# Attention with a token and channel mixer on one core: seven products in more places, tails of two pairs together, a new order of work

## The chip, the core and the metric

The kernel runs on one core of a Trainium2 chip. Its engines are TensorE (PE; the loading of its stationary operand is shown as PEld), VectorE (DVE), ScalarE (ACT), GpSimd (POOL) and SyncE (SP); POOL and SP here only issue transfers (DMA). TensorE reads from the on-chip memory SBUF and writes to eight banks of PSUM, each 128 partitions by 512 float32 columns; DVE and ACT read the banks and write results back to SBUF. Every engine works through its own list in order, and an instruction that waits holds up all that stand behind it on the same engine.

The metric is the device time of one execution in microseconds (us). The kernel before took 278.68, 279.0 and 279.62 us in three runs; the median is 279.0 us.

## The reference

There are 8 batches of 576 rows, 8 heads of 64 columns. First comes causal attention in a window of 128 rows with a distance penalty per head; then the heads are put side by side to `x` (576 by 512 per batch), and a mixer follows, first over the rows, then over the columns:

```python
scores = scale * q @ k.T + slopes * -abs(i - j)     # only where 0 <= i - j < 128
attn = softmax(scores) @ v                          # per head
x = heads of attn side by side                      # (8, 576, 512)
h = np.maximum(x.T @ w_tok1, 0.0) @ w_tok2          # 576 -> 256 -> 576
u = x + h.T
h2 = np.maximum(u @ w_ch1, 0.0) @ w_ch2             # 512 -> 1536 -> 512
out = u + h2
```

Inputs and output are float32 in HBM; the kernel computes in bfloat16 with float32 sums.

## The kernel before

A batch has 576 rows: four blocks of 128 and a tail of 64. Two batches form a pair, and the two tails of a pair share one block of 128 rows (`TAIL`). The work of batch b is in two parts. `side(b)` is everything up to `u`: transposes of q and k, `scores` (L678 on PE, exponentials on ACT at L701, masks on DVE at L711), `values` (L745, then reciprocals and scaling on DVE at L758 and L761), `token_mix` (L790, L800, L833, L829, then the addition to `ub` at L851), and the transposed copy `uT` of `u` (from batch 2 on by SP as a transposing transfer, L859). `main(b)` is the channel mixer: a first layer 512 to 1536 with ReLU into `r2`, and a second layer 1536 to 512, whose result is added to `u` and stored.

The first layer is done in 12 chunks (`chunk`, L1030): each is four matmuls of 512 columns into one bank, followed by one ReLU (ACT L1036 or DVE L1037). In batch 7 alone it is done by `unit` (L952): a unit stands for four chunks. Like Strassen's scheme it cuts the 2 by 2 blocks of the product into seven products of half size instead of eight: 28 matmuls of 256 columns instead of 16 of 512. It pays for that with sums: four differences of `uT` per batch (`halves`, L916), in each unit three copies out of PSUM (`keep`, L967), three additions (`join`, L976) and three ReLUs (L978 or L980), and the last product's own ReLU (L996). The sums of the weights are made once (`hidden_sums`, L594). `UNITS` says how many of a batch's three units are done this way: three in batch 7, none elsewhere. Batches are counted from 0 here.

The second layer of the four full blocks is done by seven products in every batch (`second`, L1218; the last product of batch 7 at L1247), with sums of `r2` on DVE (`second_sums`, L1055), sums of the weights (`weight_sums`, L576), and seven additions to `u` (L1186). The tail block of a pair is done in the odd batch: its first layer by `tail_piece` (L1073: 16 matmuls of 128 columns, three times per pair; ReLU at L1078), its second layer by 12 plain matmuls of 512 columns (L1118; in batch 7 24 of 256), then the addition at L1125 and a store.

What sets the order: `Plan` collects all operations with an estimated cost, their buffers and a rank, and simulates the five engines. Whenever an engine comes free it takes the ready operation with the smallest rank, and the order thus found is written out as the program. `side(b+1)` has ranks that lay it over the first 38% of `main(b)`. Every rank gets a random shift of at most `SHIFT` from a seed per batch (`SEEDS`). The constants `START`, `CASTS`, `LATE`, `FETCH`, `PACKET` are the planner's assumptions on transfers; they move no transfer by themselves. The order in which q, k, v and the weights are asked for in the first pair is written by hand (`LOADS`); A0 to A3 are quarters of `w_ch1`, B0 to B3 quarters of `w_ch2`, W1, P1, W2 and T0 are the token weights. All of these go through POOL's queue. Where the planner's PE is idle in the first 60 us, `emit` puts in matmuls on a zero tile (`spin`, L1302), which keep TensorE from being idle and compute nothing.

Eight banks of PSUM, six buffers `ob` (used by stores and by `keep`) and two buffers `r2` are shared out in the simulation too.

Of the kernel before, what the change touches and what calls it, by code (L numbers as in the profile page):

```python
# [64 lines left out]

class Plan:
    def __init__(self):
        self.rings, self.ops, self.orders, self.part = {}, [], 0, 0
# [7 lines left out]
    def op(self, eng, cost, emit, rank, makes=(), adds=(), part=None, uses=(), reads=(), needs=(),  # L76
# [4 lines left out]
        o = Op()  # L81
# [3 lines left out]
        o.n = len(self.ops)  # L85
        o.deps = set(many(needs))
# [31 lines left out]
    def run(self):  # L118
        ops = self.ops
        dice = [random.Random(x) for x in SEEDS]  # L120
        for o in ops:
            if SEEDS[o.part]:
                o.rank += dice[o.part].uniform(-SHIFT, SHIFT)
# [177 lines left out]
    def emit(self, spin):  # L301
# [11 lines left out]
        for _, _, go in sorted(work, key=lambda w: w[:2]):  # L313
# [23 lines left out]
SEEDS = [45795, 495947, 190309, 331881, 0, 67117, 67408, 179769, 445757]  # L337
SHIFT = 1500.0
UNIT_LATE = False
SECOND_LATE = True  # L340
# [7 lines left out]
UNITS = [0, 0, 0, 0, 0, 0, 0, 3]  # L348
# [17 lines left out]
LOADS = ("q2 k2 k1 q1 v0 W2 k8 q8 v2 v1 v3 v8 W1 q7 k7 A0 P1 k5 q5 k4 v5 "  # L366
         "q4 A1 v4 k6 q6 A2 v7 v6 A3 T0 B0 B1 B2 B3")
# [3 lines left out]
def kernel(  # L371
# [57 lines left out]
    ring("v", AHEAD, [P, H, 2 * D])  # L429
# [4 lines left out]
    ring("ub", 2, [P, NB, DM])  # L434
# [4 lines left out]
    ring("uTt", 1, [P, NCB, P])  # L439
    ring("r2", 2, [P, NHT, NC * P])  # L440
    ring("r2t", 1, [P, NHT, P])
# [98 lines left out]
    lw1, lw2, lw2t, lc1, lc2 = [], [], [], [], []  # L540
    for item in LOADS.split():
        what, n = item[:-1], int(item[-1])
        if what in ("q", "k", "v"):
            load(what, 0, n, parts_of(0, n))
        elif what == "W":
            if n == 1:
                lw1 += weights([(W1[:, 0:NC, :], w1, 512, 2080)] +
                               [(W1p[0:R, 0, :], moe_w_tok1[NC * P : S, :], 64, 210)])
            else:
                lw2 += weights([(W2[:, :, :], w2[:, :, 0 : NC * P], 256, 2630)])  # L550
        elif what == "P":
            lw1 += weights([(W1p[R:P, 1, :], moe_w_tok1[NC * P : S, :], 64, 210)])
        elif what == "T":
            lw2t += weights([(W2t[:, :, :], w2[:, :, NC * P : S], 256, 300)])
        elif what == "A":
            hs = slice(n * DCH // 4, (n + 1) * DCH // 4)
            lc1 += weights([(WC1[:, :, hs], c1[:, :, hs], 512, 2500)]) * (NHT // 4)
        else:
            js = slice(n * NHT // 4, (n + 1) * NHT // 4)
            lc2 += weights([(WC2[:, js, :], c2[:, js, :], 384, 2680)]) * (NHT // 4)  # L560
# [52 lines left out]
    qkT, xbs, ubs, r1s, uts, wides = {}, {}, {}, {}, {}, []  # L613
    turned, marks, turns = {}, {}, {}
# [159 lines left out]
    def token_mix(b, rank):  # L774
# [38 lines left out]
        uTt = plan.buf("uTt") if half else None  # L813
# [3 lines left out]
        for blk in blocks:  # L817
# [29 lines left out]
            if fold:  # L847
                plan.op("ACT", 600, lambda blk=blk, ht=ht, hs=hs: act_.copy(out=ub()[:, blk, :], in_=ht()[:, hs]),
                        rk, part=(ub, blk), uses=[ht])
            else:  # L850
                plan.op("DVE", 690, lambda blk=blk, ht=ht, hs=hs: dve_.tensor_tensor(  # L851
                    out=ub()[:, blk, :], in0=ht()[:, hs], in1=xb()[:, blk, :], op=ALU.add), rk,
                    part=(ub, blk), uses=[ht], reads=tks)
        for blk in blocks:
            if b >= FROM_U:
                def turn(blk=blk):
                    c = blk % NC
                    to = uTt()[:, :, :] if blk == TAIL else uT()[:, :, c * P : (c + 1) * P]
                    nc.sync.dma_start_transpose(out=to, in_=ub()[:, blk, :])  # L859

                turned.setdefault(b, []).append(plan.op(
                    "SP", 1200, turn, rank(0), part=(uTt if blk == TAIL else uT, blk), reads=[(ub, blk)], bus=1000))
                continue
            ut = bank()

            def go(blk=blk, ut=ut):
                for cb in range(NCB):
                    pe_.transpose(ut().bitcast(BF16)[:, cb * P : (cb + 1) * P],  # L868
                                  ub()[:, blk, cb * P : (cb + 1) * P], ident[:, :])

            def copy(blk=blk, ut=ut, eng=dve_.tensor_copy):
                c = blk % NC
# [465 lines left out]
```

## Time and profile before

| | value |
|---|---|
| runs | 278.68, 279.0, 279.62 us; median 279.0 us |
| profiled execution: span from first to last instruction | 277.5 us |
| median less that span | 1.5 us |
| mean granted TensorE clock | 0.999 |
| PE busy, share of the span | 269.9 us, 97% |
| DVE / ACT / POOL busy | 209.6 / 139.8 / 114.0 us |
| matmuls in all | 2827 |
| of these on the zero tile | 45 |

A row of groups reads: line, engine, operation, what it writes <- what it reads, shapes and count | busy us, mean ns of one | idle time before them and what ended it. Matmuls overlap, so the mean of one (379 ns for 512 columns) is its latency; what one costs in a dense stretch is read from the chain of work that ended last: so many us for so many instructions. A row of windows gives the stretch, its length, then busy time and count of PE, PEld, DVE, ACT and POOL, the granted clock, the DMA share and GB/s. In a row of the timeline stand start, duration, engine, line and operation, and in brackets the idle time before it and who ended it. In the rows of transfers the last number is the median time from issue to landing.

### The profile page before, as it was taken

To read this page: it belongs to the slowest core of one execution; us is meant where nothing else is said; L and a number is where in the kernel's file an instruction comes from. 1 tells how busy PE (TensorE), PEld (TensorE's weight loads), DVE (VectorE), ACT (ScalarE), POOL (GpSimd) and SP (SyncE) were. 2 spreads that over 40 slices of the span, in tenths; PEclk is the share of its full clock that TensorE was granted. 3 is DMA by queue.
4 is the path that set the end of the run, shared out by engine and by line. 5 is a ranking of instruction groups with operands and counts; after the bars stand their busy time and mean duration, and the time that the engine had idled before them with its cause. 6 is when DMAs were issued, how large, how long until landed. Compare 5 with 4: busy or idle time off the path is not lost.

```text
span 277.5 us, 7005 instructions
## 1 busy us (share of the span) xinstructions
PE 269.9 (97%) x2827; PEld 180.1 (65%) x2827; DVE 209.6 (76%) x497; ACT 139.8 (50%) x238; POOL 114.0 (41%) x144
## 2 busy tenths in 40 slices
PE   7899999999999999999999999999999999999994
PEld 3565765685686555595567655576667645689883
DVE  6577699978897569853989478763989549877983
ACT  5573894336960298207951096206860079105650
POOL 8889865940256037900585009600472220013000
PEclk9999999999999999999999999999999999999999
DMA  8999999999699999999899989999499750043014
GB/s 155 163 159 160 183 194 186 155 133 218 107 113 105 177 234 140 131 135 185 175 134 143 196 214 97 138 155 246 50 120 99 197 140 0 2 127 121 1 57 135
DMA packets 167553, 38.71 MB, mean 139 GB/s; under 512 B 155808, under 2 KB 166688, under 8 KB 167520
## 3 DMA queue, kind: packets, MB, share of 16 engines
q0 software_dynamic: 114032, 19.77, 92.1%
q1 hardware_dynamic: 51264, 17.83, 33.4%
q10 hardware_dynamic: 2224, 0.66, 1.2%
q8 instruction: 22, 0.36, 0.5%
q14 instruction: 11, 0.09, 0.1%
HBM read 35.85 MB, written 9.44 MB: 163 GB/s over the span
## 4 chain that ended last, share of the span: by engine, by line
PE 93%; DMA 2%; DVE 2%; ACT 1%; issue 0%; SPq 0%; DVEq 0%
PE ps L1218 26%; PE ps L1030 25%; PE ps L745 7%; PE ps L678 6%; PE ps L790 5%; PE ps L833 5%; PE ps L1073 4%; PE ps L1118 4%; PE ps L952 3%; DMA raw<-in_q_dram 2%; PE ps L1302 2%; PE ps L638 2%; PE ps L800 1%; PE ps L829 1%; PE ps L868 1%; PE ps L1015 1%
## 5 line engine op out<-in xcount | busy, mean ns | idle before, releaser
L1030 PE MATMUL ps<-uT,WC 128*128 128x512 bf16 x328 | 79.1, 379 | 0.4 <-DVE xb L761 0.4
L701 ACT ACTIVATE pe<-ps 128x1024 bf16<-128x1024 f32 (+1 forms) x76 | 63.5, 889 | 27.0 <-PE ps L678 25.7
L518 POOL DMA_DIRECT2D v<-in_v_dram x40 | 34.1, 857 | 92.7 <-PE ps L745 89.2
L1036 ACT ACTIVATE r<-ps 128x512 bf16<-128x512 f32 x75 | 44.4, 602 | 40.5 <-PE ps L1030 38.5
L1030 PEld LDWEIGHTS <-WC 128*128 128x128 bf16 x328 | 29.3, 98 | 30.1 <-issue 1.3
L711 DVE TENSOR_TENSOR pe<-pe,mask 128x1024 bf16<-128x1024 bf16 (+1 forms) x64 | 38.1, 608 | 7.2 <-ACT pe L701 6.8
L1218 PEld LDWEIGHTS <-r 128*128 128x128 bf16 x372 | 35.9, 98 | 7.2 <-issue 0.2
L518 POOL DMA_DIRECT2D qk<-in_k_dram x38 | 32.8, 870 | 3.6 <-DMA v<-in_v_dram 1.6
L518 POOL DMA_DIRECT2D qk<-in_q_dram x38 | 32.8, 868 | 2.7 <-DMA WC<-in_moe_w_ch_dram 1.0
L1218 PEld LDWEIGHTS <-s 128*128 128x128 bf16 x288 | 27.5, 98 | 6.0 <-issue 1.3
L761 DVE TENSOR_TENSOR xb<-ps,rt 128x256 bf16<-128x256 f32 (+1 forms) x72 | 29.2, 416 | 0.7
L745 PEld LDWEIGHTS <-pe 128*128 128x128 bf16 (+1 forms) x560 | 22.3, 98 | 8.7 <-DVE pe L711 2.2
L745 PE MATMUL ps<-v,pe 128*128 128x65 bf16 (+1 forms) x560 | 26.2, 194 | 0.2 <-DVE pe L711 0.2
L1218 PE MATMUL ps<-WC,r 128*128 128x256 bf16 x192 | 25.4, 273 | 0.0
L1218 PE MATMUL ps<-WT,s 128*128 128x256 bf16 x192 | 24.6, 273 | 0.0
L851 DVE TENSOR_TENSOR ub<-ps,xb 128x512 bf16<-128x512 f32 x34 | 21.2, 681 | 1.8 <-PE ps L833 1.8
L1218 PE MATMUL ps<-WT,r 128*128 128x256 bf16 x180 | 22.4, 272 | 0.0
L678 PEld LDWEIGHTS <-qkT 64*128 64x128 bf16 x560 | 14.7, 94 | 11.1 <-issue 9.4
L1186 DVE TENSOR_TENSOR raw<-ps,ub 128x512 f32<-128x512 f32 x21 | 14.3, 685 | 9.1 <-PE ps L1218 8.9
L678 PE MATMUL ps<-qkT 64*128 64x128 bf16 (+1 forms) x304 | 19.4, 216 | 0.0
L1078 ACT ACTIVATE r2t<-ps 128x512 bf16<-128x512 f32 x12 | 7.2, 603 | 22.5 <-PE ps L1073 22.5
L758 DVE RECIPROCAL rt<-ps 128x4 f32<-128x4 f32 (+1 forms) x76 | 12.4, 174 | 6.8 <-PE ps L745 6.3
(105 smaller groups left out, 350.7 us busy)
## 6 DMA issues: line engine op xcount, KB each, us to landing
out_dram<-raw SPq DMA_DIRECT2D x17, 256.0 KB, 2.6
v<-in_v_dram POOLq DMA_DIRECT2D x32, 128.0 KB, 5.4
qk<-in_q_dram POOLq DMA_DIRECT2D x30, 128.0 KB, 5.6
qk<-in_k_dram POOLq DMA_DIRECT2D x30, 128.0 KB, 5.4
WC<-in_moe_w_ch_dram POOLq DMA_DIRECT2D x8, 384.0 KB, 9.1
out_dram<-ob SPq DMA_DIRECT2D x6, 256.0 KB, 2.6
out_dram<-ob POOLq DMA_DIRECT2D x4, 256.0 KB, 3.1
out_dram<-raw POOLq DMA_DIRECT2D x4, 256.0 KB, 2.9
```

The costliest lines, as they stand in the source:

```text
L518: nc.gpsimd.dma_start(out=to()[p0 : p0 + n, :, :], in_=rows(src, b, s0, n))
L678: pe_.matmul(wide(e)[:, i, kind, a:z], lhsT=ts[kb]()[e * D : (e + 1) * D, NHP + i, :], rhs=ts[blk]()[e * D : (e + 1) * D, i, a:z], start=n ...
L701: act_.activation(out=pb()[:, e, :, lo:, c0:c1_], in_=wide(e)[:, :, lo:, c0:c1_], func=ACT.Exp, scale=scale)
L711: dve_.tensor_tensor(out=o, in0=o, in1=heads(mk, es), op=ALU.mult)
L745: pe_.matmul(view()[a:z, at, i, :], lhsT=pb()[:, e, i, kind, a:z], rhs=vb()[:, h, 0 : D + 1], start=m == 0, stop=m == len(mms) - 1, skip_g ...
L761: dve_.tensor_tensor(out=x4(), in0=view()[r0:r1_, :, :, 0:D], in1=rt()[r0:r1_, 0:n, :, :].broadcast_to([r1_ - r0, n, 4, D]), op=ALU.mult)
L790: pe_.matmul(t1[j]()[:, :], lhsT=W1[:, c, j * P : (j + 1) * P], rhs=xb()[:, blk, :], start=c == 0, stop=False)
L851: plan.op("DVE", 690, lambda blk=blk, ht=ht, hs=hs: dve_.tensor_tensor(out=ub()[:, blk, :], in0=ht()[:, hs], in1=xb()[:, blk, :], op=ALU.a ...
L1030: pe_.matmul(ct()[:, :], lhsT=WC1[:, cb, t * P : (t + 1) * P], rhs=uT()[:, cb, :], start=cb == 0, stop=cb == NCB - 1)
L1036: plan.op("ACT", 600, lambda t=t, ct=ct: act_.activation(out=r2()[:, t, :], in_=ct()[:, :], func=ACT.Relu), rk, part=(r2, t), uses=[ct], o ...
L1186: dve_.tensor_tensor(out=v, in0=both(bk), in1=src, op=ALU.add)
L1218: pe_.matmul(of(bk, c), lhsT=l(t, c), rhs=w(t), start=first, stop=g == 1 and t == HK - 1, skip_group_check=True)
```

## The change

- **Units in more batches.** `UNITS` goes from three units in batch 7 to 1, 2, 1, 2, 3 units in batches 3 to 7: nine units instead of three.
- **Tails of two pairs together.** The tails of pairs 0 and 1, and those of pairs 2 and 3, are collected in a new buffer `utl` and in a `uTt` of twice the width. `tail_piece` runs in batches 3 and 7 alone, on 256 columns: each of the 48 weight tiles of the first layer is used once for two pairs instead of once for each, in pieces of 8 matmuls of 256 columns instead of 16 of 128.
- **Second layer of the tails by seven products.** `tail_second` takes the four tail blocks as two rows of 128 and computes 7 products of 6 matmuls of 256 columns, with four sums on DVE beforehand, seven additions of 128 by 256 after them, and four stores of 64 rows on SP's queue.
- **New order.** New seeds (one for each 30 operations instead of one per batch), a higher priority (`EV`) for the additions after the second layer, other assumptions on transfers, and another order of the first loads: W2 is asked for after W1, B0 and B2 before A3, B1 right behind it, the tail's W1 rows (P1) at the end.
- The buffer of v is 96 instead of 128 columns per head.

```diff
-SEEDS = [45795, 495947, 190309, 331881, 0, 67117, 67408, 179769, 445757]
+SEEDS = {4: 978041, 5: 683284, 6: 807590, 7: 757805, 8: 512808, ...}
+GROUP = 30
+TAIL_FIRST = [False,True]
+EV = 1000.0
-UNITS = [0, 0, 0, 0, 0, 0, 0, 3]
+UNITS = [0,0,0,1,2,1,2,3]
-START = 3900.0
+START = 5200.0
-CASTS = [4800.0, 5400.0, 6000.0, 6000.0]
+CASTS = [5000.0, 5680.0, 7560.0, 8040.0]
-LATE = (2400.0, 2790.0)
-FETCH = 9500.0
+LATE = (2400.0, 3500.0)
+FETCH = 9000.0
-LOADS = ("q2 k2 k1 q1 v0 W2 k8 q8 v2 v1 v3 v8 W1 q7 k7 A0 P1 k5 q5 k4 v5 "
-         "q4 A1 v4 k6 q6 A2 v7 v6 A3 T0 B0 B1 B2 B3")
+LOADS = ("k1 q2 q1 k2 k7 v0 k8 v1 q8 v2 v3 q7 W1 v8 W2 q4 A0 "
+         "k4 k6 A1 q6 k5 v4 q5 v7 B0 A2 B2 A3 B1 v5 v6 B3 P1 T0")
-    ring("v", AHEAD, [P, H, 2 * D])
+    ring("v", AHEAD, [P, H, D + D // 2])
-    ring("ub", 2, [P, NB, DM])
+    ring("ub", 2, [P, 2 * NC, DM])
+    ring("utl", 1, [P, 2, DM])
-    ring("uTt", 1, [P, NCB, P])
+    ring("uTt", 1, [P, NCB, 2 * P])
-    ring("r2t", 1, [P, NHT, P])
+    ring("r2t", 1, [P, NHT, 2 * P])
...
         def tail_piece(t):
-            cx = bank()
...
-                for i in range(4):
-                    for cb in range(NCB):
-                        tt = t - 3 + i
-                        pe_.matmul(cx()[:, i * P : (i + 1) * P], lhsT=WC1[:, cb, tt * P : (tt + 1) * P],
-                                   rhs=uTt()[:, cb, :], start=cb == 0, stop=cb == NCB - 1)
...
+            uTt = tails_of(pr)[1]
+            for w in (t - 3, t - 1):
+                cx = bank()
...
+                    for i in range(2):
+                        for cb in range(NCB):
+                            pe_.matmul(cx()[:, 2 * i * P : 2 * (i + 1) * P], lhsT=WC1[:, cb, (w + i) * P : (w + i + 1) * P],
+                                       rhs=uTt()[:, cb, :], start=cb == 0, stop=cb == NCB - 1)
...
+        if late_tail and TAIL_FIRST[pr // 2]:
+            tail_second(b, rank, r2t)
+        second(b, rank, r2, ss, sums, ub)
+        if late_tail and not TAIL_FIRST[pr // 2]:
+            tail_second(b, rank, r2t)
+
+    def tail_second(b, rank, r2t):
+        pr = b // 2
+        utl = tails_of(pr)[0]
+        st = plan.buf("r2")
...
+        for i, f, x, y, need in (("1", ALU.add, lambda: r2t()[:, a, hi], lambda: r2t()[:, z, hi], []),
+                                 ("2", ALU.subtract, sum_of("1"), lambda: r2t()[:, a, lo], ["1"]),
+                                 ("4", ALU.subtract, lambda: r2t()[:, z, lo], sum_of("2"), ["2"]),
+                                 ("3", ALU.subtract, lambda: r2t()[:, a, lo], lambda: r2t()[:, a, hi], ["1"])):
...
+                dve_.tensor_tensor(out=o(), in0=x(), in1=y(), op=f)
...
+        for m in [1, 5, 6, 3, 2, 7, 4]:
...
+                for t in range(HK):
+                    pe_.matmul(bk()[:, 0:HN], lhsT=l(t), rhs=w(t), start=new and t == 0, stop=t == HK - 1,
+                               skip_group_check=True)
...
+                src = ob()[:, cols] if old else utl()[:, row, cols]
+                dve_.tensor_tensor(out=ob()[:, cols], in0=bk()[:, 0:HN], in1=src, op=ALU.add)
...
+                    for i in range(2):
+                        nc.sync.dma_start(out=out[4 * (pr // 2) + 2 * row + i, NC * P : S, :], in_=ob()[i * R : (i + 1) * R, :])
...
-            rk = rank(0)
+            rk = rank(0) - EV
```

Counted over the whole program, the change does this to the lists of the engines: PE 2827 to 2831 matmuls, DVE 497 to 548 instructions, ACT 240 to 261, POOL 144 to 142, SP 87 to 87.

More of the change, by code (lines that the diff above doesn't have):

```diff
@@ L1003, in main @@
         pr, half = b // 2, b % 2
-        uT, uTt, blocks = uts[b]
+        uT, blocks = uts[b]
+        late_tail = half and pr % 2
         ub = ubs[pr]
         r2 = plan.buf("r2")
-        r2t = plan.buf("r2t") if half else None
+        r2t = plan.buf("r2t") if late_tail else None
         first = []
@@ L1087, in main @@
                     second_sums(at // 6, rk)
[L1088 removed]
+                if late_tail and at % 4 == 3:
                     tail_piece(at)
```

203 lines of the change are left out of this document (122 added, 81 removed).

## The prediction

> **What bounds the kernel now.** I read the page's totals first, then who made TensorE (PE) wait, then the chain of work that ended last in order of time.
>
> ```profile
> span 277.5 us, 7005 instructions
> PE 269.9 (97%) x2827; PEld 180.1 (65%) x2827; DVE 209.6 (76%) x497; ACT 139.8 (50%) x238; POOL 114.0 (41%) x144
> PEclk9999999999999999999999999999999999999999
> PE 93%; DMA 2%; DVE 2%; ACT 1%; issue 0%; SPq 0%; DVEq 0%
> ```
>
> ```profile
> PE ps L638 <- DVE qk L533: 2.0, 3, 1.3
> PE ps L1302 <- DVE zero L482: 1.0, 1, 1.0
> PE ps L1030 <- DVE xb L761: 0.4, 1, 0.4
> PE ps L745 <- DVE pe L711: 0.2, 1, 0.2
> ```
>
> PE is busy 97% of the span, carries 93% of the chain, and these four rows are all its waits: 3.6 us, of which 3.0 lie before the first casts of q and k are done. The clock is full throughout. So after the start the kernel is one dense stream of matmuls, and what counts is how long that stream is. The chain gives the price of a matmul in the stream:
>
> ```profile
> 1.26 6.25 DMA raw<-in_q_dram
> 55.94 0.89 PE ps L1073 x16
> 59.01 2.62 PE ps L1218 x24
> 61.63 1.73 PE ps L1030 x8
> 67.58 1.83 PE ps L1030 x8
> 252.56 7.86 PE ps L952 x72
> ```
>
> A matmul of 512 columns costs 1.73 / 8 = 0.216 us, one of 256 costs 2.62 / 24 = 0.109, one of 128 costs 0.89 / 16 = 0.056. The price follows the columns, and the seven products of the first layer (L952) run at 7.86 / 72 = 0.109 as well, with no wait between them. A run of 8 that follows attention scores takes 1.83: a change of mode costs 0.10 us.
>
> **The PE stream.** The groups by shape give the counts before; those after are counted in the changed kernel's own list.
>
> ```profile
> L1030 PE MATMUL ps<-uT,WC 128*128 128x512 bf16 x328 | 79.1, 379 | 0.4 <-DVE xb L761 0.4
> L1073 PE MATMUL ps<-uTt,WC 128*128 128x128 bf16 x192 | 12.4, 219 | 0.0
> L1118 PE MATMUL ps<-WC,r2t 128*128 128x512 bf16 x36 | 8.9, 379 | 0.0
> L1118 PE MATMUL ps<-WC,r2t 128*128 128x256 bf16 x24 | 3.3, 272 | 0.0
> ```
>
> Six more units: 96 of the 328 matmuls of 512 go (20.74 us), 168 of 256 come (18.31): -2.4 us. Second layer of the tails: 36 of 512 and 24 of 256 go (7.78 + 2.62 = 10.4), 84 of 256 come (9.16): -1.2. First layer of the tails: 192 of 128 go (10.75), 96 of 256 come (10.46): -0.3. The changes of mode on PE are 100 in both lists, so nothing comes from there. Together -3.9 us. I take -3.8, since by columns alone it is 3.84.
>
> **The work that pays for it, on DVE.** Rows for one instruction of each kind:
>
> ```profile
> L916 DVE TENSOR_TENSOR tt<-uT,tt 128x512 bf16<-128x512 bf16 x2 | 0.8, 420 | 0.0
> L976 DVE TENSOR_TENSOR r<-ps,raw 128x512 bf16<-128x512 f32 x6 | 4.1, 682 | 0.8 <-ACT raw L967 0.8
> L978 DVE TENSOR_SCALAR r<-r 128x512 bf16<-128x512 bf16 x5 | 1.4, 289 | 0.1
> L1055 DVE TENSOR_TENSOR s<-r 128x768 bf16<-128x768 bf16 x16 | 8.8, 550 | 1.8 <-ACT r L1036 1.4
> L1125 DVE TENSOR_TENSOR raw<-ps,ub 128x512 f32<-128x512 f32 x2 | 1.4, 692 | 0.6 <-PE ps L1118 0.6
> L1251 DVE TENSOR_TENSOR ob<-ps,ub 128x256 f32<-128x256 f32 x1 | 0.4, 425 | 0.2 <-PE ps L1247 0.2
> L1037 DVE TENSOR_SCALAR r<-ps 128x512 bf16<-128x512 f32 x9 | 6.1, 683 | 3.4 <-PE ps L1030 2.6 <-ACT pe L701 0.8
> ```
>
> Differences of `uT` in four more batches: 16 x 0.42 = 6.7 us. Additions of the units: 18 x 0.68 = 12.3. ReLUs: 7 x 0.29 = 2.0. Sums for the tails: 8 x 0.55 = 4.4. Their additions: 14 x 0.43 = 6.0, in place of three of 0.69 and two of 0.43: +3.1. Three chunk ReLUs fewer: -2.0. Some early copies move to ACT, about -2. In all some +24.5 us: DVE goes from 209.6 to about 234 of a span near 274, 85%. ACT gets 21 more instructions at 50% load; what covers that is its idle half.
>
> DVE's room is in the stretches between one batch's addition to `u` and the next's. Here are batch 6's first layer and batch 7's attention (212.67 to 241.60), and the last batch with its three units:
>
> ```profile
> 1.00:28.91 27.91, 25.94 (x314) 15.77 (x314) 19.59 (x60) 15.60 (x28) 25.33 (x33) 1.00 1.84 167
> 212.67:241.60 28.93, 28.93 (x264) 17.45 (x262) 20.92 (x45) 13.49 (x23) 3.98 (x6) 1.00 0.33 83
> 241.60:273.53 31.93, 31.92 (x307) 27.41 (x304) 26.08 (x58) 12.68 (x35) 2.88 (x4) 1.00 0.27 82
> 273.53:277.50 3.97, 0.00 (x0) 0.00 (x0) 0.42 (x1) 0.00 (x0) 0.00 (x0) 0.96 0.37 111
> ```
>
> In the last row but one DVE carries 26.08 of 31.93 us (82%) with three units, and PE lost nothing. In batch 6's stretch two units add 2 x (3 x 0.68 + 0.3) + 1.7 = 6.4 us to 20.92, so 27.3, while PE's time falls to 28.93 - 2 x 0.43 = 28.1. That is 97%, beyond anything this trace shows over so long a stretch. Batches 4 and 5 come out near 90%. What waits behind DVE there is PE itself: a unit's last product waits for an addition, and every bank for its reader. Bound from below: 0, as in the last batch. Bound from above: in three stretches each (batches 4, 5, 6) one DVE instruction in front of two of the additions, 3 x 2 x 0.68 = 4.1. I take 0.7, one such wait in all, because 82% cost nothing and the sums still fit.
>
> So the new terms cost nothing while DVE is in time; rival B has the price if it is not.
>
> **The start.** Before, the first layer begins at 28.91; PE's last wait for a cast ends at 8.31.
>
> ```profile
> 8.31 0.78 PE L638 MATMUL ps<-ident,qk 128*128 128x128 bf16 x8 [1.34 <-DVE qk L533]
> 28.91 0.62 PE L1015 MATMUL ps<-uT,WC 128*128 128x128 bf16 x8
> 18.74 0.77 POOL L522 DMA_DIRECT2D WC<-in_moe_w_ch_dram  x1
> 30.21 0.90 POOL L522 DMA_DIRECT2D WC<-in_moe_w_ch_dram  x1
> L1302 PE MATMUL ps<-zero 128*128 128x452 bf16 (+10 forms) x45 | 11.8, 381 | 1.0 <-DVE zero L482 1.0
> ```
>
> The zero-tile matmuls go from 45 (18,712 columns) to 49 (20,712): 2000 columns, or 0.8 us at 0.216 per 512. But three groups of them now stand between the first and the last cast where PE waited before. From that last cast's transposes to the first layer the new list holds 17.9 us of stream, the old one 18.6, by the prices above (scores run in pairs on half the rows each, so at half their columns). By PE alone the first layer would start 0.6 us earlier. By the transfers it would not:
>
> ```profile
> WC<-in_moe_w_ch_dram POOLq DMA_DIRECT2D x8, 384.0 KB, 9.1
> v<-in_v_dram POOLq DMA_DIRECT2D x32, 128.0 KB, 5.4
> W<-in_moe_w_tok_dram POOLq DMA_DIRECT2D x2, 256.0 KB, 6.5
> uTt<-ub SPq DMA_TRANSPOSE x3, 4.9
> ```
>
> A0, issued at 18.74 and landing 9.1 us later at 27.8, is only just in time for 28.91, and it now stands one place further back in POOL's queue (21st instead of 20th), about 0.9 us. W2, the 19th instead of the 6th, would be issued near 17 and land near 24, where its first use stands. So I take 0 for the first layer's start, between -0.6 and +1. Behind it A3 has B0 and B2 put in front of it (768 KB) and v5, v6 and P1 taken away (288 KB). At the 167 GB/s of the first window this is 480 KB or 2.9 us later than its old landing of 30.2 + 9.1 = 39.3, thus 42, while the last chunks that need it come about a microsecond earlier than before. Bounds 0 (other chunks stand in front) and 2.9. On DVE the weight sums of B0 and B2 stand in front of masks of batch 1, so a late B2 delays attention too, within the same 2.9. I take 0.3, nearer to 0, because all the loads together are unchanged and PE did not wait for any of them before.
>
> **Small things with one answer.** The wide tail's first piece follows its transfer more closely in batch 3: some 5.4 us of stream lie between the tail's token mixing and it, and an addition (0.69), one place in SP's queue and 4.9 us of landing have to fit, so 0 to 0.8, in the 0.7 above. Four tail stores per half of the kernel now go by SP and two fewer by POOL; they stand in front of transposes whose data is not there yet: 0. The 3.97 us behind PE's last matmul hold the same two additions and stores: 0. The narrower v, the planner's assumptions and the seeds act only through the order.
>
> **The sum.** On the profiled execution: 277.5 - 3.8 + 0.7 + 0.3 = 274.7 us of span. The median of the runs lies 1.5 above this span, so 276.2 us.
>
> **The rivals.**
> A, the forecast: the shorter stream arrives with about 1 us lost on the way, 274 to 277.8.
> B, slower: the units wait for DVE. Their chain (copy, product, addition, product) stood alone in the last batch; now it runs among the masks of attention, and DVE serves its list in order. If in each of the six new units two of the steps stand behind one more DVE instruction of 0.68, it costs 6 x 2 x 0.68 = 8.2, and the time is 279.0 - 3.8 + 8.2 = 283.4. It decides from 3.8 / 6 = 0.63 us of open wait per new unit. For it: the 97% above. Against it: 82% at no cost, and the products of a unit are spread out in the new list with scores, values and token mixing between them.
> C, late loads: the full 2.9 us for A3 and B2 with DVE's 0.7: 279.0 - 3.8 + 3.6 = 278.8, no change that can be told; at half that price 277.4. For it: A0's row, which has hardly a microsecond to spare. Against it: no load made PE wait before.
> D, the change saves nothing because PE pays per pair of weight load and matmul and not per column: 348 matmuls go (96 + 60 + 192) and 348 come (168 + 84 + 96), so 279.0. Against it stand the three prices, 0.056, 0.109 and 0.216, in proportion to the columns. The Trainium skill ("TensorE: Matmul & The Clock Gate", section "Back-to-back issue gap") has such a rule: in a stream of weight loads and matmuls both set the spacing, 81 ns at 128 columns and 131 at 512. With an estimate of 98 at 256 from that page the change would save only 1.1 us, for 277.9; the trace's 216 ns at 512 does not agree.
>
> **How the numbers follow.** A 0.70, B 0.11, C 0.15, D 0.04. 0.3% (0.84 us) is about what a measurement of this kernel can tell from no change. Faster: A and 0.12 of C, short of its full price, 0.82; same: the rest of C, D and a mild B, 0.08; slower: B, 0.10. The range goes from 274.0 (DVE and loads cost nothing and the start gains 0.6: 274.6, with the runs' own spread) to 279.2, which takes in C and D; B's 283.4 is left out.
>
> **What would show it.** PE near 97% with the stream about 3.8 us shorter, waits of PE still only some microseconds; L952's successor at 0.109 per matmul in batches 3 to 6 as well. If B holds, waits of PE on the additions of the units or on banks read by DVE, between 140 and 240 us. If C holds, waits between 24 and 50 us on W2, `WC` or on masks. Wrong altogether: a granted clock below 1, or the end behind the last matmul growing from 3.97 us.

## The result, and the profile after

The changed kernel takes 278.31 us (median of 20 runs, 276.96 to 279.68); the kernel before took 278.92 beside it (20 runs, 278.62 to 280.45). The ratio is 0.9975, interval [0.9963, 0.9986]: 0.6 us or 0.25% faster, inside the 0.3% that can hardly be told from no change. The forecast was 276.2. The range held the time only because it reached up to 279.2 for rivals C and D, which both fell (below); the likeliest case did not come about. Note the spread: the kernel before varies by 1.0 us, but for one run, the changed one by 2.7.

The page of the changed kernel: span, totals, clock, and the first line of the chain that ended last.

```profile
span 277.2 us, 7065 instructions
PE 265.4 (96%) x2800; PEld 188.1 (68%) x2831; DVE 229.9 (83%) x548; ACT 148.7 (54%) x259; POOL 112.9 (41%) x142
PEclk9999999999999999999999999999999999999999
PE 78%; DVE 9%; DMA 7%; issue 2%; ACT 1%; POOL 1%; SPq 0%; DVEq 0%; POOLq 0%; ACTq 0%
```

PE's busy time fell from 269.9 to 265.4 (31 of the 2831 matmuls have no record here, so the fall looks a little larger than it is), but the span fell by only 0.3. The chain shows it too: PE carried 93% of it before and carries 78% now; DVE and DMA have 16% together. The waits of PE, complete:

```profile
PE ps L1387 <- DVE zero L496: 1.0, 1, 1.0
PE ps L1110 <- DMA uTt<-utl: 0.9, 2, 0.7
PE ps L1302 <- DVE ob L1270: 0.8, 1, 0.8
PE ps L783 <- DVE xb L799: 0.5, 1, 0.5
PE ps L1066 <- DMA uT<-ub: 0.5, 1, 0.5
PE ps L1302 <- DVE raw L1270: 0.5, 1, 0.5
PE ps L987 <- DMA uT<-ub: 0.4, 1, 0.4
PE ps L676 <- DVE qk L547: 0.2, 1, 0.2
PE ps L783 <- DVE pe L749: 0.2, 1, 0.2
PE ps L870 <- issue: 0.2, 1, 0.2
PE ps L987 <- issue: 0.2, 1, 0.2
```

Three rows name a transposing transfer directly (0.9 + 0.5 + 0.4 = 1.8 us). Two name an addition of the second layer, L1270 (0.8 + 0.5 = 1.3 us). Before, none of these five existed. The windows show where they lie: stretch, length, then busy time and count of PE, PEld, DVE, ACT and POOL, clock, DMA share, GB/s.

```profile
100.00:106.00 6.00, 5.18 (x69) 3.40 (x68) 5.78 (x14) 3.56 (x6) 5.22 (x6) 1.00 2.09 134
117.00:119.00 2.00, 1.29 (x18) 0.93 (x17) 1.34 (x3) 1.08 (x2) 0.00 (x0) 1.00 0.66 131
212.50:216.00 3.50, 2.18 (x20) 1.16 (x19) 2.26 (x6) 1.68 (x3) 1.07 (x3) 1.00 0.92 231
243.00:246.00 3.00, 2.12 (x19) 1.60 (x17) 1.73 (x5) 1.19 (x2) 0.85 (x2) 1.00 0.43 127
```

PE is idle for 0.82, 0.71, 1.32 and 0.88 us in these four, 3.7 us of 14.5; in the kernel before PE fills the same four stretches of time (with other work in them), as the sum over them shows:

```profile
sum 14.50, PE 14.50 PEld 9.29 DVE 13.00 ACT 5.84 POOL 5.56; mean PE 3.62 PEld 2.32 DVE 3.25 ACT 1.46 POOL 1.39
```

In the changed kernel DVE is full only in the first (5.78 of 6.00). In the other three it is idle for a third of the time or more: it does not lack room there, it waits. The timeline of the third stretch (start, duration, engine, line; in brackets the idle time before and who ended it) tells for what:

```profile
205.40 5.12 SPq L896 DMA_TRANSPOSE uT<-ub  x4
213.71 1.04 PE L1066 MATMUL ps<-uT,WC 128*128 128x512 bf16 x3 [0.52 <-DMA uT<-ub]
213.74 0.76 DVE L951 TENSOR_TENSOR tt<-uT 128x512 bf16<-128x512 bf16 x2 [1.46 <-DMA uT<-ub]
214.76 0.69 DVE L1270 TENSOR_TENSOR ob<-ps,ob 128x512 f32<-128x512 f32 x1
215.50 1.47 PE L1302 MATMUL ps<-WT,r 128*128 128x256 bf16 x12 [0.75 <-DVE ob L1270]
```

Batch 6 now has units, and so its differences `tt` of `uT` (`halves`, L951) stand in DVE's list. SP issues the four transposes of `uT` at about 1.28 us each (5.12 / 4) from 205.40 on. DVE comes to `tt` and stands still for 1.46 us until the transfer has landed. Behind `tt`, in the same list, stands an addition of batch 5's second layer (L1270). That addition is independent of the transfer, and its bank has to be read before the next product can go on. So PE waits twice: 0.52 for `uT` itself and 0.75 for an addition that was ready (its product, 12 matmuls from 211.39 on, was done at 212.86) and only stood in the wrong place. Near 244 the same happens once more in batch 7 (DVE idle for 1.85 us in front of `tt`, PE then for 0.46 in front of L1302). Over the whole kernel this is one row of the list of what ended DVE's idle time before the `tt` differences (us, times):

```profile
  DMA uT<-ub: 3.5, 3
```

Start and end: the first matmul of the first layer, and the last matmuls and additions.

```profile
28.17 1.07 PE L1051 MATMUL ps<-uT,WC 128*128 128x128 bf16 x16
271.33 1.47 PE L1331 MATMUL ps<-WT,r 128*128 128x256 bf16 x12
272.75 0.42 DVE L1335 TENSOR_TENSOR ob<-ps,ub 128x256 f32<-128x256 f32 x1
273.12 0.59 DVE L1379 MEMSET zero<- 128x1 bf16 x5
273.73 0.42 DVE L1335 TENSOR_TENSOR ob<-ps,ub 128x256 f32<-128x256 f32 x1
```

The first layer begins at 28.17 instead of 28.91, 0.74 earlier. PE's last matmul ends at 272.80 (271.33 + 1.47) instead of 273.53. So from the first layer to the last matmul the two kernels take the same time, 244.63 and 244.62 us: the 3.84 us taken out of the stream came back as lost time, all of it. Behind the last matmul it now takes 277.2 - 272.8 = 4.4 us instead of 3.97.

### The profile page after: what moved, and what is told of

Read it like the earlier page. It is cut to its first block, busy times and chain, and to the rows that moved or that the text cites. A ratio compares the mean times of both kernels' runs of the same rounds, so it can differ in the third digit from the quotient of the medians.

```text
span 277.2 us, 7065 instructions
## 1 busy us (share of the span) xinstructions
PE 265.4 (96%) x2800; PEld 188.1 (68%) x2831; DVE 229.9 (83%) x548; ACT 148.7 (54%) x259; POOL 112.9 (41%) x142
## 4 chain that ended last, share of the span: by engine, by line
PE 78%; DVE 9%; DMA 7%; issue 2%; ACT 1%; POOL 1%; SPq 0%; DVEq 0%; POOLq 0%; ACTq 0%
PE ps L1302 21%; PE ps L1066 16%; PE ps L987 9%; PE ps L783 6%; PE ps L716 5%; PE ps L828 4%; PE ps L870 4%; PE ps L1199 3%; PE ps L1110 3%; DMA uT<-ub 3%; DMA qk<-in_q_dram 2%; PE ps L1387 2%; DMA uTt<-utl 2%; DVE pe L749 2%; DVE s L1091 1%
## 5 line engine op out<-in xcount | busy, mean ns | idle before, releaser
L1066 PE MATMUL ps<-uT,WC 128*128 128x512 bf16 x211 | 54.1, 379 | 1.4 <-DMA uT<-ub 0.5
L1072 ACT ACTIVATE r<-ps 128x512 bf16<-128x512 f32 x54 | 31.5, 602 | 20.3 <-PE ps L1066 19.4
L1302 PEld LDWEIGHTS <-r 128*128 128x128 bf16 x372 | 35.8, 98 | 7.6 <-issue 2.1
L1066 PEld LDWEIGHTS <-WC 128*128 128x128 bf16 x232 | 20.6, 98 | 20.6 <-DMA uT<-ub 0.7
L1302 PEld LDWEIGHTS <-s 128*128 128x128 bf16 x288 | 27.7, 98 | 5.4 <-issue 0.9
L783 PEld LDWEIGHTS <-pe 128*128 128x128 bf16 (+1 forms) x560 | 22.9, 98 | 6.8 <-DVE pe L749 1.3
L1302 PE MATMUL ps<-WC,r 128*128 128x256 bf16 x192 | 24.9, 273 | 0.0
L1302 PE MATMUL ps<-WT,s 128*128 128x256 bf16 x192 | 24.3, 273 | 0.1
L1302 PE MATMUL ps<-WT,r 128*128 128x256 bf16 x180 | 22.3, 272 | 1.2 <-DVE ob L1270 0.8
L888 DVE TENSOR_TENSOR ub<-ps,xb 128x512 bf16<-128x512 f32 x30 | 19.0, 683 | 3.0 <-PE ps L870 2.9
L1270 DVE TENSOR_TENSOR raw<-ps,ub 128x512 f32<-128x512 f32 x20 | 13.7, 687 | 3.1 <-PE ps L1302 3.0
L828 PE MATMUL ps<-xb,W 128*128 128x512 bf16 x57 | 15.9, 379 | 0.3
```

The lines of the kernel that those rows point to most:

```text
L783: pe_.matmul(view()[a:z, at, i, :], lhsT=pb()[:, e, i, kind, a:z], rhs=vb()[:, h, 0 : D + 1], start=m == 0, stop=m == len(mms) - 1, skip_g ...
L828: pe_.matmul(t1[j]()[:, :], lhsT=W1[:, c, j * P : (j + 1) * P], rhs=xb()[:, blk, :], start=c == 0, stop=False)
L888: plan.op("DVE", 690, lambda blk=blk, u=u_of(pr, blk)[1], ht=ht, hs=hs: dve_.tensor_tensor(out=u(), in0=ht()[:, hs], in1=xb()[:, blk, :], ...
L1066: pe_.matmul(ct()[:, :], lhsT=WC1[:, cb, t * P : (t + 1) * P], rhs=uT()[:, cb, :], start=cb == 0, stop=cb == NCB - 1)
L1072: plan.op("ACT", 600, lambda t=t, ct=ct: act_.activation(out=r2()[:, t, :], in_=ct()[:, :], func=ACT.Relu), rk, part=(r2, t), uses=[ct], o ...
L1302: pe_.matmul(of(bk, c), lhsT=l(t, c), rhs=w(t), start=first, stop=g == 1 and t == HK - 1, skip_group_check=True)
```

## The experiments

A ratio with its interval is given against the kernel before on the same chip; it is taken over the runs and is not exactly the quotient of the two medians. The kernel before had medians of 278.82 to 278.98 in all of them, so medians of different experiments are compared directly. Beside the first four experiments it had four runs of 280.36 to 281.07, which draw their ratios down; where the ratios and the medians of two experiments say different things, the text gives both.

**The changed kernel again** (no edit; the run that the next three are compared with).

> The changed kernel once more, as the measure for the others on the same chip. Known from 20 runs: 0.9975 of the kernel before (0.9963 to 0.9986). Both theories expect 0.996 to 0.999, and the same places where TensorE stands idle: near 101 to 105, 117, 213 to 215 and 243 to 245 us, together about 3.7 us.

278.47 us (277.24 to 280.28), ratio 0.9971 [0.9945, 0.9996]. The profiled execution here has a span of 275.8, and the stall at 213 us is not in it, those near 117 and 243 are. The losses differ from run to run: the transfer lands early in one run and late in the next. That this makes the wider spread is borne out below, by the runs in which nothing waits for these transfers.

**The differences read u itself**, so that `tt` waits for no transfer; the result is then not that of the reference, and only the time is of use.

```diff
-                dve_.tensor_tensor(out=tt()[:, i - 1, :, :], in0=p(), in1=n(), op=ALU.subtract)
+                u = ubs[b // 2]()[:, b % 2 * NC + i - 1, :].rearrange("p (a b) -> p a b", a=2)
+                dve_.tensor_tensor(out=tt()[:, i - 1, :, :], in0=u, in1=tt()[:, i // 4, :, :] if i in (2, 4) else u, op=ALU.subtract)
```

> The four differences (tt) of each unit batch read u itself instead of its transposed copy: the same instructions in the same order on DVE, on the wrong data, but none of them waits for a transposing transfer. Theory T (the lost time comes from DVE standing in front of a late transposing transfer while additions that TensorE needs wait behind it): TensorE's waits on additions near 215 and 245 us go (1.3 us in the profile), only its own waits for uT stay (0.9 us); the time falls by 0.9 to 1.6 us against the changed kernel, to 0.992 to 0.9945 of the kernel before. Rival B (DVE is simply full): the amount of work on DVE is the same, no change, 0.996 to 0.999.

277.08 us (276.57 to 277.7), ratio 0.9909 [0.9877, 0.994]: 1.4 us less than the changed kernel beside it. Both waits on additions (L1270) are gone from PE's list, while those for `uTt` (1.3) and `uT` (0.6) stay. That is the 1.3 us of the rows above. All six runs lie below 9 of the 12 without the edit. (Its trace has one wait of 0.4 on `v` besides, which no other trace shows.)

**The same by order alone**: in batches 6 and 7 the differences are put behind the additions that they held up; nothing else is changed.

```diff
...
+    for b in (6, 7):
+        first = min(o.t0 for o in plan.tts[b].values())
+        over = max(o.t0 for o in plan.evs[b - 1] if first < o.t0 < first + 1500)
+        for i, o in plan.tts[b].items():
+            o.t0 = max(o.t0, over + i / 10)
```

> In batches 6 and 7 the differences stand behind the one addition of the second layer that they held up, everything else in its place; three and one DVE instructions change places. Theory T: TensorE's waits on additions near 215 and 245 us go, its waits for uT stay: 0.8 to 1.4 us less than the changed kernel, 0.9925 to 0.995 of the kernel before. Rival B: no change, 0.996 to 0.999.

277.19 us (276.63 to 277.74), ratio 0.9918 [0.9888, 0.9948]: 1.3 us less. What reading u gains is had by letting two additions pass four differences in DVE's list (three in batch 6, one in batch 7), and the spread shrinks to 1.1 us. All seven runs lie below 9 of the 12 without the edit.

**Less work for DVE, transfers as they are**: the masks of pairs 1 to 3 on half of the heads.

```diff
             def mask(es=es):
-                o = heads(pb(), es)
-                dve_.tensor_tensor(out=o, in0=o, in1=heads(mk, es), op=ALU.mult)
+                o, k = heads(pb(), es), heads(mk, es)
+                if pr >= 1:
+                    o, k = o[:, 0:2], k[:, 0:2]
+                dve_.tensor_tensor(out=o, in0=o, in1=k, op=ALU.mult)
```

> In pairs 1 to 3 the masks on DVE are applied to half of the heads only, so part of the attention is left unmasked: 0.2 to 0.3 us less on DVE in each of some 50 instructions, 10 to 13 us of DVE in all, order unchanged. Rival B (DVE is full between 60 and 240 us): most of the lost 3.7 us comes back, the time falls by 2 to 4 us, to 0.983 to 0.991 of the kernel before. Theory T: only the idle time at 101 to 105 us (0.8 us) can go; at 117, 213 and 243 us TensorE stands idle as before; 0.994 to 0.9975.

277.37 us (276.06 to 278.42), ratio 0.9918 [0.9891, 0.9945], 1.1 us less. That lies between the two expectations (at most 0.8 us for the place near 104 us alone, 2 to 4 us if DVE is full) and fits neither. The waits on `xb` and `pe` near 104 us go. Those on the additions stay, by PE's list, and so do those on `uTt` (1.1) and `uT` (0.4 and 0.2):

```profile
PE ps L1304 <- DVE ob L1272: 0.7, 1, 0.7
PE ps L1304 <- DVE raw L1272: 0.5, 1, 0.5
```

A lighter DVE does not cure the waits on additions: DVE was not busy in front of them, it was held. What the half masks do gain, near 104 us, is taken up below with the kernel in which nothing waits for transfers.

**No wait for any transposed u**, in the changed kernel and in the kernel before: every reader of the transposed u from batch 2 on reads u itself. (The differences as above; the tail's first layer, not shown, in the same way.)

```diff
...
-            return lambda cb: uT()[:, 2 * k + cb, h * HS : (h + 1) * HS]
+            return lambda cb: ubs[b // 2]()[:, b % 2 * NC + 2 * k + cb, h * HS : (h + 1) * HS]
...
-                    pe_.matmul(ct()[:, :], lhsT=WC1[:, cb, t * P : (t + 1) * P], rhs=uT()[:, cb, :],
+                    pe_.matmul(ct()[:, :], lhsT=WC1[:, cb, t * P : (t + 1) * P],
+                               rhs=ub()[:, half * NC + cb, :] if b >= FROM_U else uT()[:, cb, :],
...
```

> The changed kernel with every reader of the transposed u from batch 2 on reading u itself (wrong data, the mixer works on an untransposed u): the first layer, the units, the differences and the tail's first layer. The transposing transfers still run, nobody waits for them; every instruction and every order is kept. Theory T: all of TensorE's idle time that transfers cause goes (at 117, 213, 238 and 243 us, some 2.5 to 3 us in the profiles), the idle time near 104 us stays: 2.0 to 3.0 us less than the changed kernel, 0.986 to 0.991 of the kernel before. Rival B: at most the waits for uT themselves, 0.3 to 0.9 us, 0.994 to 0.9965.

> The same in the kernel before: every reader of the transposed u from batch 2 on reads u itself. Theory T: the kernel before did not wait for these transfers anywhere, so nothing changes: 0.998 to 1.001 of the kernel before. If transfers cost time in both kernels alike, it gains 1 us or more: below 0.997, and theory T does not explain the missing gain.

The changed kernel: 275.23 us (275.04 to 275.38), ratio 0.9865 [0.9851, 0.9878], 3.1 us less (2.0 to 3.0 were expected), as much as the five rows of waits add up to (1.8 + 1.3). The run-to-run spread falls to 0.3 us. Its waits of PE:

```profile
PE ps L1389 <- DVE zero L496: 1.0, 1, 1.0
PE ps L783 <- DVE xb L799: 0.5, 1, 0.5
PE ps L783 <- DVE pe L749: 0.2, 1, 0.2
```

The kernel before: 278.94, ratio 1.0006 [0.9995, 1.0018]. There the same transfers cost nothing. So it is not the transfers as such, but what the change put behind them and how soon.

**Neither late transfers nor the full load on DVE**: the last edit and the half masks together.

> Both at once: the readers of the transposed u read u itself from batch 2 on, and in pairs 1 to 3 the masks cover half of the heads. What is left of the missing gain after the transfers (275.2 us) is put to DVE's load. If DVE's load is the rest, the idle 0.5 us near 104 us goes and the time falls by 0.4 to 1.0 us to 0.983 to 0.985 of the kernel before, which is the forecast stream with the earlier start and nothing lost. If DVE's load costs nothing beside the transfers: 0.986 to 0.987.

274.01 us (273.87 to 274.12), ratio 0.9824 [0.9811, 0.9836]: 1.2 us less than without the half masks, a little more than the 0.4 to 1.0 expected.

A page and PE's waits of this kernel:

```profile
span 272.2 us, 7091 instructions
PE 266.2 (98%) x2831; PEld 187.8 (69%) x2831; DVE 219.1 (80%) x548; ACT 148.6 (55%) x259; POOL 113.0 (42%) x142
```

```profile
PE ps L1391 <- DVE zero L496: 1.0, 1, 1.0
PE ps L676 <- DVE qk L547: 0.5, 2, 0.3
```

Both waits lie ahead of the first layer; once it has begun PE waits for nothing. This kernel runs the changed stream, all 2831 matmuls, without a gap, and so gives the worth of the stream by itself: 274.01 against 278.9, 4.9 us. From the forecast's 3.84, the 0.74 of the earlier start, the 0.6 us of waits that the kernel before had itself (the `xb` and `pe` rows in the prediction) and 0.4 of the longer end, one expects 278.9 - 3.84 - 0.74 - 0.6 + 0.4 = 274.1. (By the two traces, 277.5 and 272.2, the difference is 5.3, 0.5 more than these terms; the agreement to 0.1 is partly luck.)

The last 1.2 us, from 275.23 to 274.01, are what the full masks cost on DVE, and 1.1 of them lie in one place. In the kernel without transfer waits the 16 matmuls of `values` before that place start at 98.27, with the half masks as well at 98.06; the next token mixing starts here, first without and then with the half masks:

```profile
111.04 0.59 PE L870 MATMUL ps<-r,W 128*128 128x512 bf16 x2
109.73 0.59 PE L872 MATMUL ps<-r,W 128*128 128x512 bf16 x2
```

The same work takes 12.77 us in one and 11.67 in the other. In the changed kernel this stretch is 12.77 long too, and 11.67 with the half masks alone; it is where DVE was full (5.78 of 6.00). PE's list names only 0.7 of the 1.1, the waits on `xb` and `pe`; the rest lies in gaps too short for it.

**The tails alone**: units as before, order planned anew with the changed kernel's seeds.

```diff
-UNITS = [0,0,0,1,2,1,2,3]
+UNITS = [0, 0, 0, 0, 0, 0, 0, 3]
```

> The changed kernel with units only in batch 7, as before; the tails, the loads and the seeds as in the changed kernel. The planner makes another order from it, one that nobody has tuned, so its time has idle time of its own on top. The stream on TensorE is 2.4 us longer than the changed kernel's and 1.5 shorter than the kernel before. If the units are what costs the gain (rival B), it is not slower than the changed kernel: 0.993 to 0.998. If order and transfers decide (theory T), it is slower than the changed kernel by its longer stream and by the untuned order: 1.000 to 1.015.

281.86 us (280.58 to 282.22), ratio 1.0107 [1.0092, 1.0123], slower than both kernels. PE's longest waits are two on an addition of the second layer (L1270), 2.3 us together.

This does not measure the tails. The seeds shift the ranks of another list of operations here, and the order that comes out has its own stalls. The parts of the change could not be taken apart this way, and the units alone were not run for the same reason. By its columns this stream is 2.4 us longer than the changed kernel's; the time is 3.5 us longer, so this order loses some 1.1 us more than the changed kernel's, although it has fewer units. It does not show that the units cost nothing.

**The tail first**: the order with `tt` behind, and in batches 3 and 7 the tail's token mixing, addition and transposing transfer ahead of those of the four blocks.

```diff
...
+    for b in (3, 7):
+        for e in ("PE", "DVE", "SP"):
+            *others, tail = plan.tl[b, e]
+            at = min(o.t0 for o in others) - 0.1
...
+            tail.t0 = at
```

> As the kernel with the differences behind the addition, and in batches 3 and 7 the tail goes first on its way to the mixer: its token mixing, its addition on DVE and its transposing transfer stand in front of those of the full blocks (two to four matmuls, one to two additions and one transfer change places). Theory T: TensorE's wait for the tail's transfer near 117 us (0.8 us) goes, that near 238 us (0.3 us) as well: 0.5 to 1.1 us less than the kernel with the differences behind the addition, 0.988 to 0.9915 of the kernel before. Rival B (DVE is full, not late): no gain over that kernel, 0.9915 to 0.993.

276.47 us (276.15 to 277.1), ratio 0.9912 [0.9899, 0.9926], 0.7 us under the one without it. By the ratios, 0.9912 and 0.9918, the difference is 0.2 us, within the intervals, so the size is not settled; the trace settles the wait itself. The wait for `uTt` is gone from PE's list. In the changed kernel's timeline the tail's addition, its transfer and the first piece stood like this:

```profile
112.23 0.68 DVE L888 TENSOR_TENSOR utl<-ps,xb 128x512 bf16<-128x512 f32 x1
113.66 1.24 SPq L896 DMA_TRANSPOSE uTt<-utl  x1
118.34 1.03 PE L1110 MATMUL ps<-uTt,WC 128*128 128x256 bf16 x8 [0.71 <-DMA uTt<-utl]
```

and with the tail first:

```profile
111.57 0.69 DVE L890 TENSOR_TENSOR utl<-ps,xb 128x512 bf16<-128x512 f32 x1
112.29 1.19 SPq L899 DMA_TRANSPOSE uTt<-utl  x1
117.50 1.03 PE L1114 MATMUL ps<-uTt,WC 128*128 128x256 bf16 x8
```

The addition ended at 112.91 and SP took the transfer only at 113.66, since other transposes stood in front; now it starts 0.03 us behind the addition.

**Transposes on two queues**: in batches 6 and 7 two of the four transposes of `uT` go by ACT's queue, on top of the last order.

```diff
-                def turn(u=u, to=to):
-                    nc.sync.dma_start_transpose(out=to(), in_=u())
+                def turn(u=u, to=to, blk=blk):
+                    q_ = nc.scalar if b in (6, 7) and blk % NC % 2 and blk != TAIL else nc.sync
+                    q_.dma_start_transpose(out=to(), in_=u())
...
+    for b in (6, 7):
+        for i in (1, 3):
+            plan.tl[b, "SP"][i].t0 = plan.tl[b, "DVE"][i].t0 + 1
```

The last lines put the two behind the additions whose results they read.

> A version with the full computation: as the kernel with the tail first, and in batches 6 and 7 two of the four transposing transfers of u are issued by ACT instead of SP, so the last of the four is issued some 2.5 us earlier. Theory T with the issue time on SP (1.2 to 1.3 us each) as what makes them late: the waits for uT near 213 and 243 us (0.4 and 0.2 us) go, 0.3 to 0.8 us less than the kernel with the tail first, 0.9885 to 0.9905 of the kernel before. If the landing itself (2.3 to 4.6 us) makes them late and not the queue, no gain: 0.991 to 0.992.

281.6 us (280.39 to 284.43), ratio 1.0112 [1.0071, 1.0154]: 5 us slower; both expectations (0.3 to 0.8 us faster, or no gain) missed. PE's longest waits, then the timeline of the queues in batch 6:

```profile
PE ps L992 <- DVE tt L956: 2.3, 1, 2.3
PE ps L1308 <- ACT r L1036: 2.1, 1, 2.1
```

```profile
204.84 7.46 SPq L900 DMA_TRANSPOSE uT<-ub  x2
207.32 1.28 ACTq L900 DMA_TRANSPOSE uT<-ub  x1
208.73 1.20 ACTq L900 DMA_TRANSPOSE uT<-ub  x1
```

Two transposes on SP span 7.46 us where four took 5.12, because SP waits for the transfers on ACT's queue to land. The row of SP's own queue:

```profile
SPq L900 <- DMA uT<-ub: 10.8, 2, 5.8
```

On ACT the transposes also stand in front of a ReLU: ACT is idle for 4.22 us before it (until 208.65), and PE waits 2.1 us for its `r`. The differences `tt` come later too, and PE waits 2.3 us for them. The Trainium skill ("DMA: Bandwidth & Descriptors", section "Silent corruption: two transposing streams in flight at once") says that transposes of two queues have to be kept apart by waiting for full completion. In this trace they are kept apart, and the price is the 10.8 us of waiting above; no run here shows what happens without the wait.

**DVE's list near 102 us**, on top of that: two instructions that nobody needs soon (one sum, one copy) behind one that PE waits for.

```diff
...
+    by = {o.n: o for o in plan.ops}
+    for i, n in enumerate((564, 665)):
...
+        by[n].t0 = by[658].t0 + 1 + i
```

> As the kernel with two queues, and near 102 us two DVE instructions that nobody waits for yet (a sum of r2, 0.55 us, and the copy of the tail rows, 0.5 to 0.7 us) stand behind the masks and the scaling that TensorE waits for, instead of in front. If the idle time near 104 us comes from DVE's queue order: 0.4 to 0.8 us less than the kernel with two queues, 0.986 to 0.989 of the kernel before; if from masks that are late by themselves: no change.

281.53 us (281.17 to 282.86), ratio 1.0104 [1.0087, 1.0122]. The wait on `xb` near 104 us is gone, but the median says nothing beside the loss to the two queues. So the same move without them:

> The order of e7 with every transpose on SP's queue again, and near 102 us two DVE instructions that nobody needs soon (one of the sums for the tails and one early copy) moved behind one that TensorE waits for; the results are computed in full. Theory (late transposes and DVE's queue are separate terms): the half microsecond of TensorE's wait for the casts of xb near 104 us goes, as it did when the same move was made together with two queues, and the time is 0.4 to 0.8 us under e7's, ratio 0.9880 to 0.9900. Rival (the queue is merely full, and what is moved back is waited for later): the same as e7, 0.9905 to 0.992.

276.13 us (275.7 to 276.55), ratio 0.9904 [0.9887, 0.992]. That is 0.34 us less than the order with the tail first, between what the theory and the rival gave, and the intervals overlap. By the trace the wait on `xb` has gone: the stretch from the `values` at 98 us to the tail's token mixing near 111 is 12.18 us long instead of 12.87, 0.69 less, with the same work on DVE. So of the 1.1 us that the half masks gave there, 0.7 is order and not load. Behind it a wait of 0.3 for `uTt` is back, which the kernel with the tail first did not have. By the time it is not settled how much of the 0.69 stays.

**The end**: the two groups of memsets (they write a column of the zero tile, which no matmul reads any more by then) in front of earlier additions, into DVE's idle time, on top of the last.

```diff
+    for n, x in ((1465, 1433), (1464, 1454)):
...
+        by[n].t0 = by[x].t0 + 1
```

> The order of e13 with the two groups of five one-column memsets, which stand between VectorE's last three additions (0.59 us each, 269.09 and 270.04 of e13's trace), moved in front of earlier additions, into stretches where VectorE is idle for 0.61 and 0.89 us; the results are computed in full. Theory (the end behind TensorE's last matmul grew from 3.97 to 4.4 us because the last addition stands behind the second group): the end goes back to 3.9 to 4.0 us and the time falls by 0.3 to 0.6 us against e13, 275.5 to 275.9, ratio 0.987 to 0.9895. Rival (the last addition waits for something else, or the store takes longer): no change, ratio 0.990 to 0.992.

275.05 us (274.3 to 275.38), ratio 0.9852 [0.9824, 0.988], 1.1 us less, more than expected. The end of its timeline:

```profile
267.40 1.47 PE L1336 MATMUL ps<-WT,r 128*128 128x256 bf16 x12
268.25 0.42 DVE L1340 TENSOR_TENSOR ob<-ps,ub 128x256 f32<-128x256 f32 x1
268.91 0.42 DVE L1340 TENSOR_TENSOR ob<-ps,ub 128x256 f32<-128x256 f32 x1 [0.23 <-PE ps L1336]
```

The last addition starts 0.04 us behind PE's last matmul (268.87), as in the kernel before, instead of 0.93. With a span of 272.5 the end is 272.5 - 268.87 = 3.63 us, where it was 4.4. That explains some 0.75 of the 1.1 us; the rest is not explained, and PE's waits for transfers happen to be 0.4 us shorter in this trace than in the one of the kernel without the move. This version beats both kernels: by 3.8 us the one before, by 3.3 us the changed one, with the same work on every engine, only in another order.

## Why the prediction failed

**The bound and the stream: right.** PE bounds the kernel, and the price of a matmul follows its columns. The changed stream without gaps comes out at 274.01 where the forecast's terms with the measured start and end give 274.1. PE's busy time, with every record in both traces, falls by 3.7 us (269.9 to 266.2), four more matmuls on the zero tile included. The units run at 0.109 us per matmul in the new batches too, by the chain of the changed kernel in batch 6:

```profile
221.61 2.18 PE ps L987 x20
```

So the stream did get shorter by about the forecast's 3.84 us.

**Rival D: fell.** If PE paid per pair of weight load and matmul, the stream would have saved 0, or 1.1 us by the prediction's estimate from the Trainium skill's figures; it saved about 3.8. The Trainium skill's spacing ("TensorE: Matmul & The Clock Gate", section "Back-to-back issue gap") does not hold for this kernel, where 512 columns cost 0.216 us and 256 cost 0.109.

**The start: 0 forecast, 0.74 earlier measured.** PE alone set it, as the lower bound said (-0.6). The transfers did not hold it: A0 was issued at 18.0 in the changed kernel, not later than before (18.74), although it stands one place further back. So the 0.9 us charged for that place was wrong.

**Rival C, late loads: fell.** PE's list has no wait on weights, and none between 24 and 50 us. The 0.3 was 0.

**DVE: its amount about right, its price wrong. This is the step that failed.** 234 us forecast, 229.9 measured. But the prediction asked of DVE only whether it has room: "82% cost nothing and the sums still fit", hence one wait of 0.7. It priced the differences of `uT` as 16 x 0.42 us of work, and did not name what they wait for. They are among the first readers of the transposing transfers and stand in the same list as the additions that PE needs next. The row for their wait could have been looked for: the transfers' row for `uT`, 3.1 us from issue to landing, four in a row on SP at more than a microsecond each, was not among the rows used. Measured in its place:

| lost after the first layer's start | forecast | measured | by |
|---|---|---|---|
| additions held up behind `tt` | 0 | 1.3 | reading u, or moving `tt` back |
| PE itself waits for `uT` and `uTt` | 0 to 0.8, in the 0.7 | 1.8 | the three rows of waits; all transfers together 3.1 |
| DVE's list near 104 us (load and order) | 0.7 | 1.2 | half masks without transfers; 0.7 of it by order alone |
| together | 0.7 | 4.3 | 278.31 - 274.01 |

The upper bound set for DVE, 4.1 us, was near the measured 4.3, by another mechanism; that is luck. Batch 3's transfer of the tails, a small thing with one answer in the prediction (0 to 0.8), cost 0.7 and belonged into the sum as a term of its own.

**Rival B: its place right in part, its mechanism wrong.** It said that steps of the units would stand behind a busy DVE between 140 and 240 us, 8.2 us. PE's two waits on additions lie at 215 and 245. What stood behind DVE were the additions of the second layer of the batch before, and DVE was idle in front of them. The half masks, which left those waits where they were, tell the two apart. Where DVE was busy and PE waited for it, near 104 us, batch 2 is in the mixer, which has no units.

**The end: 0 forecast, 0.4 longer.** "The same two additions and stores" left out two groups of memsets of 0.59 us each, one of which the new order put between them; the kernel before has both (at 269.3 and 269.9) ahead of its last four additions, where DVE had time. The prediction had named a longer end as a sign of being wrong altogether; it came, but it is the small part.

Together: 279.0 - 3.84 - 0.74 + 0.4 for stream, start and end gives 274.8; 4.3 of waits, less the 0.6 that the kernel before had itself, gives 278.5, against 278.31. Since the 4.3 is itself taken from measured times, this shows that the terms close; it is no second proof. One more term was slightly off: the prediction added 1.5 us from the span to the time, and the runs lie 1.7 to 1.8 above their own spans.

## What to carry to other kernels

When an instruction is added to a list that runs in order, ask first what it waits for and only then how long it takes: behind a waiting transfer every independent instruction of that engine waits too, and the engine's busy share shows nothing of it. If an idle stretch of an engine ends with a transfer, and the next engine then waits for that engine, move the waiting instruction back in the list before making the transfer faster. When a stream gets shorter, every transfer that it covered must be set against the new distance between its issue and its first reader.

## What was not expected of the hardware

The 24 transposing transfers of `uT`, from issue to landing in the kernel before, and then in the changed one:

```profile
DMA to landing us min/median/max: 2.3/3.1/6.0
```

```profile
DMA to landing us min/median/max: 2.3/3.3/7.6
```

The medians are close, the longest are not. What waits for them makes the time spread from run to run: 2.7 us over the 20 runs of the changed kernel, 0.3 over the four and the five runs in which nothing waits for them, with the same work on PE. Splitting them over two queues, which by the waits in the program do not transpose at the same time, made the kernel slower, not faster.
